# Step 1 of a batched FFT kernel: three fp16 products of a 98x98 matrix replaced by four 49x49 fp32 quarters of a folded input

## The chip, the cores and the metric

The kernel runs on one core of a Trainium2 chip. Its engines work side by side, each through its own fixed list of instructions: TensorE (PE in the profile) for matmuls, VectorE (DVE), ScalarE (ACT) and GpSimd (POOL) for elementwise work, and SyncE (SP), whose queue issues nearly all DMAs here. The metric is the device time of one execution in microseconds.

## What is computed

Eight batches of 3136 x 256 numbers go through a real FFT along the 3136 axis, a complex 256x256 mix with a bias, a soft threshold, the inverse FFT, and then a token-wise block with two matmuls (256 to 1024 and back):

```python
X = np.fft.rfft(x, axis=1)                      # x: (8, 3136, 256)
Yr = Xr @ w_r - Xi @ w_i + b_r
Yi = Xr @ w_i + Xi @ w_r + b_i
Y  = soft(Yr, 0.01) + 1j * soft(Yi, 0.01)       # sign(v) * max(|v| - 0.01, 0)
y  = np.fft.irfft(Y, n=3136, axis=1)
h  = y @ w_in;  sm = softmax(h);  solu = h * sm
out = (layernorm(solu) * g_ln) @ w_out
```

## The kernel before

3136 is 98 x 32, and the transform is done in two steps. **Step 1** multiplies x, seen as 98 rows (n1) of 32 x 256 columns, by a 98x98 matrix of cosines and sines. **Step 2** (`fwd2`) multiplies, for every pair of frequencies, by a 64-row matrix that holds the twiddle factors. The mix (`mix`), the threshold, step 3 (`inv1`, the inverse of step 2) and step 4 (`inv2`, the inverse of step 1) follow; between steps 1 and 2 and between 3 and 4 the numbers go through DRAM (`s1`, `s2`) to be turned. The token block is `moe_head` (first matmul, softmax), `moe_turn` (split into two fp16 parts, transposed by DMA) and `moe_tail` (second matmul, output).

Precision near fp32 is had from fp16 matmuls: a number is split into a high and a low half, and three products are added (high by high, low by high, high by low). A number must be scaled first so that fp16 holds it. So for batches three to eight (`b >= PLAIN`, which is 2) x is read twice: `load_peak` (L567) reads it in eight pieces of 128x784 to find its largest value, `x_scale` (L574) makes a power of two of it, and `fwd1` (L636) reads it again in eight chunks of 98x1024, splits each on ACT (`xh`) and DVE (`xl`), multiplies both halves of 512 columns three times by the matrix `fa16_s`, splits each product again on ACT and DVE into `av`, and stores it as fp16 pairs. `load_bin` (L702) then brings those pairs in ready for step 2. Batches one and two take `fwd1_plain` (L664): x is read once, multiplied in fp32 by `fa_s` with no scale, and the split is made after step 1, in `load_bin`.

Engines' lists are not in the order of the code. The kernel records every operation with a key (`nc.key`) and its needs; a planner (`Plan.order`, L365) walks through modelled time, and at each moment an engine takes, of the operations that could start within 50 ns of the first, the one with the lowest key. `weigh` (L319) sets an operation's modelled length: for TensorE it is divided by the number of array pieces that work at once (`op.half`: 2 for step 2, 8 for step 3). `banks` (L492) shares PSUM's eight banks out: `front_psum` and `inv2` use the name `pf` with at most five, `moe_head` `ph` with five, `moe_tail` `po` with two. All operations are issued by one helper line, so the profile's rows have L363 throughout, and groups are told apart by their tiles. Keys of step 1 come from `front_a` (L1282), those of steps 2 and 3 from `front_b` (L1292), from numbers at the end of the kernel.

In the rows `xt` is x as loaded, `bin` the input of step 2, `fb` and `gb` the matrices of steps 2 and 3, `w_hi`, `Xh` and `Xl` the mix, `th` and `tl` the two halves of the token block's transposed activations, `pf`, `ph` and `po` PSUM.

## Time and profile before

| | us |
|---|---|
| median of 3 runs | 1533.49 (1532.99 to 1537.09) |
| span of the profiled execution, first to last instruction | 1529.5 |
| PE busy | 1500.7 (98%) |
| DVE busy | 1285.7 (84%) |
| ACT busy | 1240.2 (81%) |
| POOL busy | 1143.4 (75%) |

The profile gives no time for its execution beyond the span, so the span stands for it: it is 4.0 us below the median of the runs, which is what lies around it there (start and end of the execution). A busy share is an average over the span; the same engine can be idle in one stretch and full in another, which the views by stretch show. Matmuls overlap, and their ends are modelled: how long one takes in a stream is read from the distance between starts, not from its duration.

### The profile page before, as it was taken

The numbers are of one execution on the slowest core, as the hardware profiler recorded it, in microseconds if no ns is written. First come the engines' busy times: TensorE is split into PE (matmuls) and PEld (weight loads), VectorE is DVE, ScalarE is ACT, GpSimd is POOL, SyncE is SP. The second block draws the span as 40 slices with busy tenths as digits, with TensorE's granted clock in tenths as the row PEclk, the third lists the DMA queues.
The fourth block names the chain that finished last, engine by engine and source line by source line (L and its number), as shares of the span: only waits on it lengthen the run. The fifth ranks groups of instructions, "written<-read, shape, count | busy, mean of one in ns | idle before, by whom it ended". The sixth has DMA issues, their size and how long they took to land.

```text
span 1529.5 us, 42136 instructions
## 1 busy us (share of the span) xinstructions
PE 1500.7 (98%) x15375; PEld 1061.3 (69%) x15375; DVE 1285.7 (84%) x3076; ACT 1240.2 (81%) x2532; POOL 1143.4 (75%) x1848
## 2 busy tenths in 40 slices
PE   6979999999999999999999999999999999999998
PEld 3436777677766777677766777667776677766766
DVE  5898898989898998989889898898979888776764
ACT  6778887987898778987888877897879788788886
POOL 0558987778966887678876788668986699867776
PEclk8989999999999999999999999999999999999999
DMA  8789866998699976999869996799969976687766
GB/s 267 219 265 211 166 129 128 254 222 222 131 216 233 224 165 127 235 230 227 155 140 238 232 202 143 160 236 230 199 135 201 208 161 121 138 173 141 149 124 115
DMA packets 531588, 285.69 MB, mean 187 GB/s; under 512 B 426500, under 2 KB 504688, under 8 KB 531380
## 3 DMA queue, kind: packets, MB, share of 16 engines
q1 hardware_dynamic: 530932, 281.39, 83.6%
q8 instruction: 120, 1.97, 0.5%
q10 hardware_dynamic: 448, 1.61, 0.4%
q14 instruction: 88, 0.72, 0.1%
HBM read 103.07 MB, written 77.07 MB: 118 GB/s over the span
## 4 chain that ended last, share of the span: by engine, by line
PE 86%; DVE 5%; ACT 3%; DMA 2%; POOL 2%; issue 1%; SPq 0%; DVEq 0%; ACTq 0%; POOLq 0%
PE ph L363 30%; PE po L363 30%; PE pf L363 24%; PE pb L363 2%; DMA tl<-ll 1%; DVE u L363 1%; DMA u<-in_x_dram 1%; DVE xl L363 1%; DVE nm L363 1%; ACT u L363 1%; DMA s<-av 0%; POOL ll L363 0%; DVE peaks L363 0%; SPq L363 0%; ACT lh L363 0%
## 5 line engine op out<-in xcount | busy, mean ns | idle before, releaser
L363 POOL TENSOR_TENSOR ll<-u,lh 128x1024 f16<-128x1024 f32 x196 | 421.4, 2150 | 103.7 <-ACT lh L363 96.0
L363 PE MATMUL po<-wout,th 128*128 128x256 f16 x3136 | 374.5, 273 | 0.0
L363 ACT ACTIVATE u<-ph,m,hsb 128x512 f32<-128x512 f32 x384 | 297.1, 780 | 80.6 <-DVE m L363 79.7
L363 PEld LDWEIGHTS <-th 128*128 128x128 f16 x3136 | 303.9, 98 | 58.7 <-issue 1.8
L363 DVE TENSOR_REDUCE nm<-ph 128x1 f32<-128x512 f32 x392 | 266.0, 688 | 89.2 <-PE ph L363 87.0
L363 DVE SCALAR_TENSOR_TENSOR u<-ph,ch,u 128x512 f32<-128x512 f32 x392 | 285.5, 748 | 46.9 <-ACT u L363 36.9
L363 PE MATMUL ph<-win_hi,ring_hi 128*128 128x512 f16 x768 | 291.3, 379 | 0.4 <-DVE u L363 0.3
L363 PE MATMUL ph<-win_low,ring_lo 128*128 128x512 f16 x768 | 291.0, 379 | 0.0
L363 PE MATMUL ph<-win_lo,ring_hi 128*128 128x512 f16 x768 | 291.0, 379 | 0.0
L363 ACT CAST lh<-u 128x1024 f16<-128x1024 f32 x196 | 206.5, 1054 | 67.1 <-DVE u L363 63.9
L363 PEld LDWEIGHTS <-ring_hi 128*128 128x128 f16 x1536 | 148.6, 98 | 138.1 <-issue 2.2
L363 ACT ACTIVATE junk<-u,total 128x1024 bf16<-128x1024 f32 x196 | 227.4, 1160 | 9.5 <-POOL total L363 8.4
L363 PE MATMUL po<-wout,tl 128*128 128x256 f16 x1568 | 203.4, 273 | 1.3 <-DMA tl<-ll 1.3
L363 PEld LDWEIGHTS <-tl 128*128 128x128 f16 x1568 | 151.7, 98 | 27.6 <-DMA tl<-ll 2.8
L363 POOL TENSOR_TENSOR y<-yt,yc 128x512 f32<-128x512 f32 (+1 forms) x104 | 132.0, 1274 | 26.1 <-DVE yc L363 20.7
L363 PE MATMUL pf<-w_hi,Xh 128*128 128x256 f16 x532 | 145.0, 273 | 0.1
L363 PE MATMUL pf<-w_hi,Xl 128*128 128x256 f16 x532 | 145.0, 273 | 0.0
L363 PE MATMUL pf<-w_lo,Xh 128*128 128x256 f16 x532 | 145.0, 273 | 0.0
L363 PEld LDWEIGHTS <-ring_lo 128*128 128x128 f16 x768 | 75.1, 98 | 90.7 <-DVE ring_lo L363 0.2
L363 PEld LDWEIGHTS <-Xh 128*128 128x128 f16 x1168 | 113.2, 98 | 35.5 <-issue 5.7
L363 POOL TENSOR_TENSOR yl<-y,yh 128x512 f16<-128x512 f32 x96 | 112.7, 1178 | 17.7 <-ACT yh L363 17.4
L363 POOL TENSOR_TENSOR r<-r,mhalf 128x1 f32<-128x1 f32 x196 | 113.2, 578 | 12.6
(204 smaller groups left out, 2699.0 us busy)
## 6 DMA issues: line engine op xcount, KB each, us to landing
xt<-in_x_dram SPq DMA_DIRECT2D x104, 392.0 KB
zt<-s SPq DMA_DIRECT2D x56, 392.0 KB
s<-zout SPq DMA_DIRECT2D x42, 512.0 KB
s<-av SPq DMA_DIRECT2D x48, 392.0 KB
bin<-s SPq DMA_DIRECT2D x36, 512.0 KB
out_dram<-o SPq DMA_DIRECT2D x128, 96.0 KB
out_dram<-o SPq DMA_DIRECT2D x136, 64.0 KB
out_dram<-o SPq DMA_DIRECT2D x128, 32.0 KB
```

What stands on the lines that cost most here:

```text
L363: getattr(engine, name)(*args, **kw)
```

## The change

From batch three on step 1 becomes `fwd1_fold`. A cosine row of the 98x98 matrix has the same value at n and n + 49 for an even frequency and the opposite one for an odd frequency; so has a sine row. The rows n and n + 49 of x are therefore added (`both`) and subtracted (written over the second half of `xf`), and each result is multiplied by a 49x49 matrix of its own (`fq_s`), in fp32 and without a scale. Two chunks of 1024 columns are taken together: four half chunks of 512 columns, each with a sum and a difference, make eight matmuls, and these are placed in four 64x64 pieces of the array by `tile_position`. The products leave PSUM by one ACT copy for each bank of 512 columns and are stored in fp32 (128 rows, of which 98 are used). `load_bin` and `fwd2_last` take the form that batches one and two have: they load fp32 and split it on ACT and DVE, now from two DMAs (four for `bin_s`) for one. `load_peak` is gone: the largest value is found in `xf`, and `x_scale` comes after step 1. x is loaded in 48 + 1 rows for each of two half chunks, four DMAs a chunk, into four buffers `xf` that stay in place; `clear_pads` fills the unused rows 49 to 63 and 113 to 127 of them once. `bin` has four buffers, where it had three.

The keys are new throughout: one table by kind of work, shifts by batch and kind (`SHIFT`) and by tile (`ROLE`), and modelled matmul lengths 0.6% longer.

```diff
+    FQ = np.zeros((4 * N2, 2, 2 * N2))
+    for odd in range(2):
+        for c in range(H):
+            k1, im = (2 * (c // 2) + 2 - odd, c % 2) if c < 2 * Q else (H * odd, 0)
+            t = 2 * np.pi * ((np.arange(H) * k1) % N1) / N1
+            for r in range(2):
+                FQ[r * 2 * N2 : r * 2 * N2 + H, odd, c] = -np.sin(t) if im else np.cos(t)
...
+KEYS = {
+    "fa": -300, "bias": -162.48, "start": 0, "warm": -200, "plain": -200, "weights": -161.13, "consts": -100,
...
+SHIFT = {
+    "inv24": 0.3, "inv21": 0.73, "a3": 0.8, "inv25": -0.83, "inv22": -2.27, "a5": 2.48, "a2": -3.15,
...
-            op.half = 8 if "gb" in ins[0].tile.kw["name"] else 2 if moving.tile.kw["name"][:2] == "fb" else 0
-            op.length += n / max(op.half, 1)
+            op.half = 8 if "gb" in lhs else 4 if lhs == "fq_s" else 2 if moving.tile.kw["name"][:2] == "fb" else 0
+            op.length += self.PACE * n / max(op.half, 1)
...
-    def fwd1(b, c):
...
+    def fwd1_fold(b, c0):
+        if c0 == 0:
+            s1[b] = dram.tile([P, N2, D], F32, name="s1")
+        half, rows = 2 * N2, 2 * N2 + H
+        v = x[b].rearrange("(h p n) d -> p h (n d)", h=2, n=N2)
...
+        for c in (c0, c0 + 1):
+            xt = xf[c % 4].rearrange("p (h m) -> p h m", h=2)
+            for r in range(2):
+                ms = slice(c * C1 + r * HF, c * C1 + (r + 1) * HF)
+                for p, n in ((0, H - 1), (H - 1, 1)):
+                    nc.sync.dma_start(xt[r * half + p : r * half + p + n], v[p : p + n, :, ms])
+            note_peak(b, c, NCH, xf[c % 4][:rows])
+            both = xp.tile([P, HF], F32, name="both")[:rows]
+            nc.vector.tensor_add(both, xt[:rows, 0], xt[:rows, 1])
+            nc.vector.tensor_sub(xt[:rows, 1], xt[:rows, 0], xt[:rows, 1])
+            folds.append((both, xt[:rows, 1]))
+        avs = [xp.tile([P, C1], F32, name="av", bufs=2) for _ in folds]
+        pas = [[front_psum(b) for _ in range(2)] for _ in folds]
+        nc.reserve(*avs)
+        with nc.together():
+            for fold, pa in zip(folds, pas):
+                for r in range(2):
+                    for odd in range(2):
+                        nc.tensor.matmul(
+                            pa[r][odd * half : (odd + 1) * half],
+                            fq_s[r * half : r * half + H, odd],
+                            fold[odd][r * half : r * half + H],
+                            start=True,
+                            stop=True,
+                            tile_position=(r * half, odd * half),
+                        )
+        for c, av, pa in zip((c0, c0 + 1), avs, pas):
+            for r in range(2):
+                nc.scalar.copy(av[:, r * HF : (r + 1) * HF], pa[r])
+            nc.sync.dma_start(s1[b][:, c * n2 : (c + 1) * n2], av.rearrange("p (n d) -> p n d", d=D))
...
-            t = fp.tile([P, QG, 2, D], F16, name="bin", bufs=3)
-            nc.sync.dma_start(t.rearrange("p q t d -> p q (t d)"), v[:, g * QG : (g + 1) * QG])
-            return t
...
+            t = fp.tile([P, QG, D], F32, name="bin", bufs=4)
+            half = 2 * N2
+            for odd in range(2):
...
+                nc.sync.dma_start(t[(1 - odd) * half : (2 - odd) * half], v[:, g * QG : (g + 1) * QG])
...
-        steps = [(load_peak, (b, c)) for c in range(NPK)] + [(x_scale, (b,))] + [(fwd1, (b, c)) for c in range(NCH)]
+        steps = [(fwd1_fold, (b, c)) for c in range(0, NCH, 2)] + [(x_scale, (b,))]
```

How the lists move is shown at one place of three engines, before and then after; an "x2" stands for that many equal rows. On PE, the first chunk of step 1 of batch three before, as it stands between a first token matmul (`ph`) and the mix: six products with `fa_s` (the fp16 matrix `fa16_s`), each with its weight load.

```order
L363 MATMUL pf<-xh,fa_s 98x512
L363 LDWEIGHTS fa_s
L363 MATMUL pf<-xh,fa_s 98x512
L363 LDWEIGHTS fa_s
L363 MATMUL pf<-xl,fa_s 98x512
L363 LDWEIGHTS fa_s
L363 MATMUL pf<-xh,fa_s 98x512
L363 LDWEIGHTS fa_s
L363 MATMUL pf<-xh,fa_s 98x512
L363 LDWEIGHTS fa_s
L363 MATMUL pf<-xl,fa_s 98x512
L363 LDWEIGHTS Xh_4384
```

Now, at the second group of step 1 by the new list, behind the second matmul of a token tile (`po`); a fp32 matmul is one row here that brings its own weights.

```order
L422 LDWEIGHTS tl
L422 MATMUL po<-wout,tl 128x256
L422 MATMUL pf<-both,fq_s 64x512
L422 MATMUL pf<-xf_101,fq_s 64x512
L422 MATMUL pf<-both,fq_s 64x512
L422 MATMUL pf<-xf_101,fq_s 64x512
L422 MATMUL pf<-both,fq_s 64x512
L422 MATMUL pf<-xf_118,fq_s 64x512
L422 MATMUL pf<-both,fq_s 64x512
L422 MATMUL pf<-xf_118,fq_s 64x512
L422 LDWEIGHTS Xh_3827
L422 MATMUL pf<-w_hi,Xh_3827 128x256
```

Two chunks are one group of eight rows where one chunk was six rows and as many weight loads; `both` and the difference (`xf`) alternate, first rows 0 to 48 of the array and then 64 to 112, and the same four pieces once more for the second chunk.

On DVE, in the middle of step 1 of batch three before, with rows of the token block (`u`, `nm`, `m`, `ch`) between them.

```order
L363 SCALAR_TENSOR_TENSOR xl<-xt,sc,xh 98x1024
L363 TENSOR_SCALAR ch<-m 128x1
L363 TENSOR_SCALAR ch<-ch,hsb 128x1
L363 SCALAR_TENSOR_TENSOR u,su_7861<-ph,ch,u 128x512
L363 SCALAR_TENSOR_TENSOR u,su_7870<-ph,ch,u 128x512
L363 SCALAR_TENSOR_TENSOR av<-pf,av 98x2x256 x2
L363 SCALAR_TENSOR_TENSOR xl<-xt,sc,xh 98x1024
L363 TENSOR_REDUCE nm<-ph 128x1 x2
```

And now at the last pair of chunks of step 1 of a batch.

```order
L422 TENSOR_REDUCE peaks<-xf_118 113x1
L422 SCALAR_TENSOR_TENSOR u,su_8351<-ph,ch,u 128x512
L422 TENSOR_TENSOR both<-xf_101 113x512
L422 TENSOR_REDUCE top<-peaks 113x1
L422 TENSOR_TENSOR xf_101<-xf_101 113x512
L422 TENSOR_TENSOR both<-xf_118 113x512
L422 TENSOR_REDUCE nm<-ph 128x1
L422 TENSOR_TENSOR xf_118<-xf_118 113x512
```

The splits of x (`xl`) and of the product (`av`) have left; the reduction for the largest value (`peaks`), the sum and the difference stand there, and `x_scale` (`top`) behind the last reduction.

On SP's queue before, where x of the next batch is read for its largest value and for step 1 and `bin` is loaded between them.

```order
L363 DMA xt<-in_x_dram 128x784 x3
L363 DMA_TRANSPOSE tl<-ll 128x8x128
L363 DMA bin<-s_7995 128x4x512
L363 DMA_TRANSPOSE th<-lh 128x8x128
L363 DMA bin_s<-s_7995 64x256 x2
L363 DMA xt<-in_x_dram 128x784
L363 DMA out_dram<-o 64x256 x2
L363 DMA xt<-in_x_dram 98x1024
```

And now, at the end of the loads of one batch and the start of its `bin`.

```order
L422 DMA xf_86<-in_x_dram 48x2x512
L422 DMA xf_86<-in_x_dram 1x2x512
L422 DMA s_6129<-av 128x1024
L422 DMA xf_86<-in_x_dram 48x2x512
L422 DMA s_6129<-av 128x1024
L422 DMA xf_86<-in_x_dram 1x2x512
L422 DMA_TRANSPOSE th<-lh 128x8x128
L422 DMA out_dram<-o 64x256 x2
L422 DMA_TRANSPOSE tl<-ll 128x8x128
L422 DMA zt<-s_6847 98x2048 x2
L422 DMA_TRANSPOSE th<-lh 128x8x128
L422 DMA bin<-s_6129 64x4x256 x2
```

A chunk of x is two rows of 48 and two of 1 partition where it was one row and one for the peak, and a `bin` is two rows of 64 partitions where it was one of 128.

## Rows read from the trace of the kernel before

**Rows 1.** The page of the kernel before: busy time of each engine with its share of the span, and two rows of the forty slices (PE's busy tenths, and the granted TensorE clock in tenths of full speed).
```profile
PE 1500.7 (98%) x15375; PEld 1061.3 (69%) x15375; DVE 1285.7 (84%) x3076; ACT 1240.2 (81%) x2532; POOL 1143.4 (75%) x1848
...
PE   6979999999999999999999999999999999999998
...
PEclk8989999999999999999999999999999999999999
```

**Rows 2.** The page's chain of work that ended last: shares of the span by engine.
```profile
PE 86%; DVE 5%; ACT 3%; DMA 2%; POOL 2%; issue 1%; SPq 0%; DVEq 0%; ACTq 0%; POOLq 0%
```

**Rows 3.** Stretches of the span, all engines: start:end and length in us, then busy us of PE, PEld (weight loads), DVE, ACT and POOL with their numbers of instructions, the granted clock, the mean busy share of the 16 DMA engines and GB/s.
```profile
0.00:100.00 100.00, 84.31 (x843) 41.42 (x844) 75.89 (x146) 71.68 (x136) 42.34 (x41) 0.91 0.78 240
100.00:200.00 100.00, 93.18 (x804) 67.08 (x803) 87.03 (x223) 80.02 (x171) 79.36 (x122) 0.97 0.92 203
...
800.00:900.00 100.00, 99.81 (x1030) 71.57 (x1029) 93.67 (x206) 81.92 (x169) 74.18 (x118) 1.00 1.07 242
...
1400.00:1529.00 129.00, 124.54 (x964) 87.50 (x961) 80.43 (x216) 98.96 (x200) 90.04 (x178) 0.99 0.71 131
```

**Rows 4.** PE's instructions in order of time around the first chunk of step 1 of batch three, and the two that follow it (start us, us until the modelled end of the last, operation, shapes, number of instructions).
```profile
256.52 0.60 PE L363 MATMUL pf<-xh,fa_s 98*98 98x512 f16 x2
256.96 0.38 PE L363 MATMUL pf<-xl,fa_s 98*98 98x512 f16 x1
257.17 0.59 PE L363 MATMUL pf<-xh,fa_s 98*98 98x512 f16 x2
...
257.82 0.27 PE L363 MATMUL pf<-w_hi,Xh 128*128 128x256 f16 x1
...
259.13 1.91 PE L363 MATMUL po<-wout,th 128*128 128x256 f16 x16
```

**Rows 5.** The same view of PE at one chunk of step 1 of batch two, which is already multiplied in fp32 (two matmuls of 512 columns, which the trace records as four), and the next instruction.
```profile
57.14 1.88 PE L363 MATMUL pf<-xt,fa_s 98*98 98x512 f32 x4
58.86 0.38 PE L363 MATMUL pb<-w_hi,Xh 128*128 128x512 f16 x1
```

**Rows 6.** The same view of PE at a group of step 3 (tile `gb`, 96 matmuls on eight 32x64 pieces of the array; its first 16 and last 16) and what follows it, then at a group of step 2 (tile `fb`, 96 matmuls of 64 columns on two 64-row pieces) with the rows on both sides.
```profile
260.97 0.42 PE L363 MATMUL pf<-yh,gb 32*64 32x256 f16 x16
...
262.08 0.40 PE L363 MATMUL pf<-yh,gb 32*64 32x256 f16 x16
262.42 1.05 PE L363 MATMUL po<-wout,tl 128*128 128x256 f16 x8
...
514.83 1.91 PE L363 MATMUL po<-wout,th 128*128 128x256 f16 x16
516.67 1.57 PE L363 MATMUL pf<-fb,bin 64*128 64x64 f16 x96
518.17 1.05 PE L363 MATMUL po<-wout,tl 128*128 128x256 f16 x8
```

**Rows 7.** DVE's instructions grouped by operation and shape: out<-in, out shape<-in shape, number, busy us in all and mean ns of one, idle time before them.
```profile
L363 DVE SCALAR_TENSOR_TENSOR xl<-xt,sc,xh 98x1024 f16<-98x1024 f32 x48 | 64.9, 1351 | 0.1
L363 DVE SCALAR_TENSOR_TENSOR av<-pf,av 98x512 f16<-98x512 f32 x96 | 63.0, 686 | 7.1 <-ACT av L363 7.1
L363 DVE TENSOR_REDUCE peaks<-xt 128x1 f32<-128x784 f32 x48 | 46.0, 962 | 0.1
L363 DVE TENSOR_REDUCE peaks<-xt 98x1 f32<-98x1024 f32 x12 | 14.5, 1210 | 9.3 <-DMA xt<-in_x_dram 9.3
L363 DVE SCALAR_TENSOR_TENSOR bin<-bin,sc 128x1024 f16<-128x1024 f32 x6 | 8.1, 1356 | 0.4 <-ACT bin L363 0.4
L363 DVE SCALAR_TENSOR_TENSOR u<-u,junk 128x512 f32<-128x512 uint32 x4 | 2.7, 683 | 0.0
L363 DVE SCALAR_TENSOR_TENSOR bin_s<-bin_s,sc,bin_s 64x256 f16<-64x256 f32 x2 | 1.0, 484 | 0.1
L363 DVE TENSOR_SCALAR un<-pf 128x2 f32<-128x2 f32 x7 | 1.1, 159 | 4.8 <-PE pf L363 4.7
```

**Rows 8.** The same view of ACT.
```profile
L363 ACT ACTIVATE xh<-xt,sc 98x1024 f16<-98x1024 f32 x48 | 54.9, 1162 | 1.2 <-DVE sc L363 1.1
L363 ACT ACTIVATE av<-pf 98x512 f16<-98x512 f32 x96 | 54.6, 603 | 4.7 <-PE pf L363 3.1 <-DMA s<-av 0.9
L363 ACT COPY av<-pf 98x512 f32<-98x512 f32 x16 | 9.0, 586 | 1.9 <-PE pf L363 1.1 <-DMA s1f<-av 0.8
L363 ACT ACTIVATE bin<-bin,sc 128x1024 f16<-128x1024 f32 x6 | 7.2, 1197 | 0.0
L363 ACT ACTIVATE bin_s<-bin_s,sc 128x256 f16<-128x256 f32 x2 | 1.2, 598 | 0.0
```

**Rows 9.** The same view of PE: the matmuls of step 1 on the second half of x, and the last column tells what PE waited for before them in the whole run.
```profile
L363 PE MATMUL pf<-xl,fa_s 98*98 98x512 f16 x96 | 36.3, 378 | 0.6 <-DVE xl L363 0.6
```

**Rows 10.** DMA: the page's count of packets; issues by tile with their number and size; and, from the views of the tiles `xt` and `tl`, the time that one issue takes on SP's queue (ns min/median/max).
```profile
DMA packets 531588, 285.69 MB, mean 187 GB/s; under 512 B 426500, under 2 KB 504688, under 8 KB 531380
...
xt<-in_x_dram SPq DMA_DIRECT2D x104, 392.0 KB
s<-av SPq DMA_DIRECT2D x48, 392.0 KB
...
L363 SPq DMA_DIRECT2D xt<-in_x_dram x104: 316/500/1904, 46.5 to 1172.8; - x104
...
L363 SPq DMA_TRANSPOSE tl<-ll x196: 1231/1248/3634, 134.7 to 1521.2; - x196
```

More of the change, by code (lines that the diff above doesn't have):

```diff
@@ L241, in tile @@
         return View(t, (0, 128), np.arange(512), F32)
+KEYS = {
+    "fa": -300, "bias": -162.48, "start": 0, "warm": -200, "plain": -200, "weights": -161.13, "consts": -100,
+    "groups": 0, "x0": -197.18, "y0": -78.59, "b0": -110.81, "b0s": 7.792, "w_in0": -138.86, "w_in1": -62.72,
+    "w_in": -46.29, "w_out0": -26.19, "w_out": -16.44, "mix": 13.09, "pads": -16.1, "a1": -43.04, "a1s": 5.385,
+    "a2": 4.85, "a2s": 4.919, "a": 4.52, "b1": 3.41, "b1s": 0.904, "b": -21.55, "bs": 1.176, "inv2": -2.03,
+    "turn": 12.26, "tail": 4.37, "as": 3.466,
+}
@@ L244, with first_tile, key_of, __init__ @@
+def first_tile(b):
+    return 24 * b + b // 2
+def key_of(stage, b=0, n=0, keys=KEYS):
+    if stage in ("a", "b"):
+        name = f"{stage}{b}" if f"{stage}{b}" in keys else stage
+        step = keys[f"{name}s"]
+        at = first_tile(b - 1 if stage == "b" else b - 2) if b > (stage == "a") else 0
+        return at + keys[name] + n * step
+    if stage in ("inv2", "head", "turn", "tail"):
+        return first_tile(b) + n + keys.get(stage, 0)
+    return keys[stage]
 class Op:
-    def __init__(self, engine, key, seq):
-        self.engine, self.key, self.seq = engine, key, seq
+    def __init__(self, engine, stage, role, seq):
+        self.engine, self.stage, self.seq = engine, stage, seq
+        self.key = key_of(*stage) + SHIFT.get("".join(map(str, stage[:2])), 0) + ROLE.get(f"{stage[0]}/{role}", 0)
@@ L271, in __init__, with at @@
     def __init__(self, nc):
-        self.nc, self.ops, self.key, self.group, self.held, self.reserved = nc, [], 0.0, None, (), ()
+        self.nc, self.ops, self.stage, self.group, self.held, self.reserved = nc, [], ("start",), None, (), ()
         for e in self.ENGINES:
             setattr(self, e, _Engine(self, e))
+    def at(self, *stage):
+        self.stage = stage
     def together(self):
@@ L290, in take @@
         if op is None or op is True:
-            op = Op(engine, self.key, len(self.ops))
+            role = args[0].tile.kw["name"] if isinstance(args[0], View) else "out"
+            op = Op(engine, self.stage, "D" * (name == "dma_start") + role, len(self.ops))
             self.ops.append(op)
@@ L472, in fft_mix_solu_kernel @@
 @with_exitstack
-def fft_mix_solu_kernel(ctx: ExitStack, tc, x, w_r, w_i, b_r, b_i, w_in, w_out, g_ln, fa, iaf, fa16, fb, fs, gb, gs, ia, out):
+def fft_mix_solu_kernel(ctx: ExitStack, tc, x, w_r, w_i, b_r, b_i, w_in, w_out, g_ln, fa, fq, none, iaf, fb, fs, gb, gs, ia, out):
     nc = Plan(tc.nc)
@@ L510, in fft_mix_solu_kernel @@
         nc.sync.dma_start(bias_row[:, r], v.unsqueeze(0))
-    nc.key = 0
+    nc.at("start")
     ident = const.tile([P, P], F32, name="ident")
@@ L558, in load_after @@
         nc.sync.dma_start(t, src)
+    xf = [const.tile([P, C1], F32, name=f"xf{i}") for i in range(4)]
     peaks, scales = {}, {}
@@ new lines, in clear_pads @@
+    def clear_pads():
+        for t in xf:
+            for r in (0, 2 * N2):
+                nc.sync.dma_start(t[r + H : r + 2 * N2], none)
+    def fwd1_fold(b, c0):
[3 more added lines that the diff above has]
+        v = x[b].rearrange("(h p n) d -> p h (n d)", h=2, n=N2)
+        n2 = C1 // D
+        folds = []
+        for c in (c0, c0 + 1):
[28 more added lines that the diff above has]
+            nc.sync.dma_start(s1[b][:, c * n2 : (c + 1) * n2], av.rearrange("p (n d) -> p n d", d=D))
@@ L669, in fwd1_plain @@
         n2 = C1 // D
-        pool, name, bufs = (mp, "u", 4) if b == 0 and c % 2 == 0 else (xp, "xt", 4)
-        xt = pool.tile([P, C1], F32, name=name, bufs=bufs)[:N1]
-        if b and c < 4:
-            nc.hold(raw[0, 4])
+        if b:
+            xt = xf[c % 4][:N1]
+            if c < 4:
+                nc.hold(raw[0, 4])
+        else:
+            xt = xf[c // 2][:N1] if c % 2 else mp.tile([P, C1], F32, name="u", bufs=4)[:N1]
         queue = nc.scalar if b == 0 and c % 2 else nc.sync
@@ L1192, in fft_mix_solu_kernel @@
     iaf_s = const.tile([N1, N1], F32, name="iaf_s")
-    fa16_s = const.tile([N1, 2, N1], F16, name="fa16_s")
+    fq_s = const.tile([P, 2, 2 * N2], F32, name="fq_s")
     ia_s = const.tile([N1, 3, N1], F16, name="ia_s")
-    nc.key = 0
+    nc.at("groups")
     fb_s, gb_s = {}, {}
@@ L1297, in front_b @@
         for n in range(NU + lag):
-            nc.key = key + n * step
+            nc.at("b", b, n)
             for fn, m in ((fwd2, n), (mix, n - 1)):
```

147 lines of the change are left out of this document (66 added, 81 removed).

## The prediction

> **What bounds the kernel now.** I read the busy times first: PE is busy 1500.7 of 1529.5 us, no other engine over 84% [rows 1]. Then the chain of work that ended last: 86% of it is PE [rows 2]. Then the stretches: PE misses 15.7 us of the first 100 us and 6.8 of the second, from there at most a few tenths in 100 us, at the full granted clock, and 4.5 us at the end; that makes 22.5 of its 28.8 idle us in the first 200 [rows 1, 3]. So behind 200 us a microsecond of PE's work that goes, or comes, moves the end by a microsecond, unless another engine fills the place; the fullest, DVE, reaches 93.7 in the stretch from 800 to 900 us [rows 3]. PE does not wait on step 1's inputs either: before the matmuls of `xl` it lost 0.6 us in the whole run [rows 9]. The question is thus what step 1 costs PE before and after.
>
> A single profiled execution gives these rows: span 1529.5 us. The median of the runs is 1533.49, so I add each sum to 1533.5 and take the 4.0 us around the span as unchanged.
>
> **PE, removed.** One chunk of step 1 (six fp16 matmuls of 512 columns) goes from 256.52 to 257.82 us, where the mix begins: 1.30 us [rows 4]. Two chunks, which the change takes together, are 2.60 us; six batches of four pairs make 24 pairs: 62.4 us.
>
> **PE, added.** fp32 stands in the trace on the whole array: two matmuls of 98x98 by 512 columns from 57.14 to 58.86 us, 1.72 us, recorded as four passes of 0.43 us, so 0.86 us for one matmul [rows 5]. A pair now has eight matmuls of 512 columns on four pieces of the array. If the four pieces stream side by side, each has two: 2 x 0.86 = 1.72 us.
>
> No row shows fp32 in pieces, but two show fp16 in them. Twelve matmuls of 256 columns go from 257.82 to 259.13 us, 0.109 us each [rows 4]. The 96 of a step 3 group would take 10.5 us in single file; they take 1.45 us, 260.97 to 262.42 [rows 6]. Eight abreast they are twelve deep, 1.31 us, and 0.14 us is left over at the way out; 16 matmuls from 259.13 end at 260.87, so another 0.10 us is lost at the way in [rows 4, 6]. Step 2, two abreast: 96 of 64 columns are 48 deep at a quarter of 0.109, 1.31 us, and take 1.50 (516.67 to 518.17); the way in is 0.10 again (16 from 514.83 end at 516.57), so 0.29 us in all against 0.24 [rows 6]. Between the two I take 0.26 us for a group on four pieces.
>
> New group: 1.72 + 0.26 = 1.98 us. Saved: 2.60 - 1.98 = 0.62 us, 24 times: 14.9 us.
>
> Both ends of the unknown: perfect overlap with no switching cost is 1.72 us a pair, a gain of 21.1 us; eight matmuls in single file are 6.88 + 0.26 = 7.14 us, a loss of 109 us. I take four abreast, because the nearest rows (pieces of the same array, of 32 and of 64 rows) run at their full number abreast. One thing differs, and it decides the first rival below: in steps 2 and 3 neighbouring matmuls go to different pieces, while a fp32 matmul is two passes [rows 5], and both must go to the same piece.
>
> **DVE.** Removed: 46.0 (peaks of 784 columns) + 64.9 (`xl`) + 63.0 (`av`) = 173.9 us [rows 7]. Added: 48 reductions of 1024 columns at 1.21 = 58.1; 96 sums and differences of 512 columns, which no row shows, at 0.68 by the nearest, a two-input fp32 instruction of 512 columns, = 65.6; 36 splits of `bin` at 1.356 = 48.8; 6 of `bin_s` at 0.484 = 2.9 [rows 7]. Together 175.4 us: 1.5 more, beside PE. For the sums and differences the ends are 0.48 us (half of a 784-column reduction) and 0.69 (`av`, which reads PSUM), so DVE's total changes by -18 to +2 us over six batches, none of it on the path while DVE has 6 us in 100 free in its fullest stretch [rows 3, 7].
>
> **ACT.** Removed 54.9 + 54.6 = 109.5 us; added 96 copies at 0.586 (56.3), 36 `bin` at 1.197 (43.1), 6 `bin_s` at 0.598 (3.6): 103.0 us, 6.5 less [rows 8]. POOL gets no instruction and loses none.
>
> **DMA and SP's queue.** x is read once: 48 loads of 392 KB go, 19.3 MB; the fp32 store has 128 rows where 98 stood, 120 KB more in each of 48, 5.9 MB. Net -13.4 of 285.7 MB [rows 10]. Issues: per batch 32 loads of x for 16, 12 of `bin` for 6, 4 of `bin_s` for 2, so 24 more, 144 for six batches, and 8 for the pads: 152 at 0.50 us = 76 us more on SP, whose transposes take 392 x 1.25 = 490 us of the 1529 [rows 10]. What is queued behind a late issue there is a transpose, and behind that the second token matmul on PE. A thousand other issues at 0.50 us would still leave SP over 500 us of the span, so I price it at nothing; without that cover a transpose is late by the four issues of a chunk, 2 us. Whether loads in 2 KB runs take longer to land than in 4 KB runs no row shows; between a gain of a few us (the stretch from 800 to 900 us has its DMA engines full, 1.07 [rows 3]) and a loss of as many I take nothing.
>
> **What moves.** Step 1 no longer waits for the scale, and `x_scale` comes behind it. Its small DVE-PE-DVE steps (`un` waited 4.8 us for PE in seven batches [rows 7]) now stand ahead of the first `bin` split. The lists put a stretch of token work there, which hides them; bare, they would cost about 1 us a batch, 6 us. The first group of step 1 of batch three stands much earlier on PE, in the stretch where PE has holes. With new keys those 22.5 idle us can shrink or grow; the rows give no direction, so nothing in the sum, and up to half of them, 11 us, either way in the range. No stall is removed after 200 us; what would be late next is DVE, whose share rises by the 1% that the span shrinks.
>
> **Sum.** 1533.5 - 14.9 = 1518.6 us.
>
> **Rival 1, the two passes hold the line (slower).** If PE starts matmuls strictly in their order, the second pass of a matmul waits for the first on its piece, and the next matmul, though its piece is free, waits behind. Then each matmul sets the line back by one pass: 8 x 0.43 + 0.43 = 3.87, with the switch 4.13 us a pair, 1.53 more than before, 24 times 36.7 us: 1570.2 us. It decides as soon as a pair takes over 2.60 us, which is fewer than three pieces abreast. For it: the order `both`, difference, `both`, difference gives no two passes of different pieces as neighbours but at the seams. Against it: pieces 32 and 64 rows high run at their full number here [rows 6].
>
> The Trainium skill speaks on both sides. "TensorE: Matmul & The Clock Gate" (Part 3, The mechanism) says that matmuls start and end in program order, with no reordering, and that only weight loads are pulled ahead; taken literally, that is this rival and 1570 us. "TensorEngine Tiling (Array Packing)" (Key Properties) says that tiles run independently and load and multiply in parallel; that is the forecast. The rows of steps 2 and 3 agree with both, since no piece is used twice in a row there.
>
> **Rival 2, the gain is given back in waits (about the same).** A group now takes four of the five `pf` banks at once and holds them through four ACT copies of 0.59 us, where a half chunk took one [rows 8]; its eight matmuls start only when two chunks are summed and differenced. If the mix or step 4 behind it waits 0.62 us for each group, the gain is gone: 1533.5; at 0.9 us it is 1540. For it: DVE and ACT are over 80% full, and ACT's `av` waited for PE only 3.1 us, so the banks are turned over tightly [rows 1, 8]. Against it: step 3 takes four banks already, and PE shows no idle time around its group [rows 6].
>
> **Rival 3, no pieces at all.** fp32 in single file: 1533.5 + 109 = 1642 us. Only a rule against fp32 in pieces would do it; no row speaks for it.
>
> **Chances.** A change of 0.3% (4.6 us) is about what a measurement of this kernel can tell from none. Forecast 0.66, with its own range 1505 to 1528: the low end is the sum less half of the early idle time and some of the switching cost, the high end a few tenths of wait a group. Rival 1 0.16, rival 2 0.14 (1527 to 1540), rival 3 0.01, and 0.03 for an early stretch that loses more than all the rest gains. The range 1505 to 1540 holds the forecast and rival 2, some 0.80; rival 1 lies outside. Faster (under 1528.9): the forecast and a little of rival 2, 0.69. Within 0.3%: most of rival 2, 0.11. Slower: rivals 1 and 3 and the rest, 0.20.
>
> **What the profile after will show.** Right: a group of 16 passes on `fq_s` (eight matmuls) between its first start and the next instruction's in 1.9 to 2.1 us; PE busy near 1486 us and its idle time still under 30 us; DVE within 5 us of 1286, ACT some 6 under 1240; 272 MB moved. Wrong by rival 1: 4.1 us a group with starts 0.43 us apart. Wrong by rival 2: groups of 2.0 us, with idle time of PE in front of them or behind them, put down to ACT `av` or DVE `xf`. Most directly, the forecast falls if a group takes over 2.6 us.

## The result, and the profile after

The changed kernel takes 1544.3 us (median of 4 runs, 1542.6 to 1544.5) where the kernel before takes 1533.4 beside it: ratio 1.0069, 95% interval 1.0054 to 1.0084. It is 0.7% slower. The forecast was 1518.6 us, 1% faster, and the range ended at 1540. All ratios below are to runs of the kernel before on the same chip, 1532.0 to 1533.0 us each time, with their 95% interval behind them; two ratios whose intervals overlap are not told apart. One execution of `e11_x64_bin1` (1724.4 us) and one of `e18_single3` (3130.2 us) took far longer than the others of the same kernel and are left out of what is given for these two.

The page of the kernel after, busy time and DMA packets; its span is 1542.3 us.
```profile
PE 1495.1 (97%) x15471; PEld 1036.9 (67%) x15471; DVE 1299.9 (84%) x3070; ACT 1228.4 (80%) x2526; POOL 1164.0 (75%) x1848
...
DMA packets 533014, 273.26 MB, mean 177 GB/s; under 512 B 427676, under 2 KB 505992, under 8 KB 532804
```
PE is busy 5.6 us less than in [rows 1] and idle 47.2 us instead of 28.8. The bytes fell by 12.4 MB [rows 10]. So the kernel moves less, multiplies less and takes longer: the loss is waiting.

PE after, in order of time, at one group of step 1 (two chunks, eight matmuls, recorded as 16 passes; this answers to [rows 4, 5]), and the token matmul that follows.
```profile
442.45 0.64 PE L422 MATMUL pf<-both,fq_s 49*64 49x512 f32 x1
442.45 0.64 PE L422 MATMUL pf<-xf,fq_s 49*64 49x512 f32 x1
442.46 0.64 PE L422 MATMUL pf<-both,fq_s 49*64 49x512 f32 x1
442.47 0.64 PE L422 MATMUL pf<-xf,fq_s 49*64 49x512 f32 x1
442.93 0.59 PE L422 MATMUL pf<-both,fq_s 49*64 49x512 f32 x1
...
443.36 0.59 PE L422 MATMUL pf<-both,fq_s 49*64 49x512 f32 x1
...
443.79 0.59 PE L422 MATMUL pf<-both,fq_s 49*64 49x512 f32 x1
...
444.33 0.39 PE L422 MATMUL ph<-win_hi,ring_hi 128*128 128x512 f16 x1
```
Four passes start within 20 ns, then four more, four times over; the next instruction starts 1.88 us after the first. So it is in 23 of the 24 groups; one takes 1.94 us.

The stretches after, columns as in [rows 3]: then the same two stretches before, and of the run without the added DMAs (`e17_noone_bin1`, below).
```profile
150.00:400.00 250.00, 245.98 (x2680) 177.75 (x2679) 219.63 (x508) 205.17 (x418) 205.47 (x313) 1.00 0.82 178
400.00:1250.00 850.00, 835.45 (x8937) 583.47 (x8936) 744.27 (x1763) 686.30 (x1423) 660.23 (x1055) 1.00 0.85 181
```
```profile
150.00:400.00 250.00, 249.44 (x2862) 184.73 (x2860) 223.31 (x519) 207.32 (x429) 206.71 (x313) 1.00 0.84 183
400.00:1250.00 850.00, 849.02 (x8917) 610.67 (x8916) 747.79 (x1785) 705.56 (x1444) 651.68 (x1060) 1.00 0.89 194
```
```profile
150.00:400.00 250.00, 246.35 (x2687) 178.33 (x2686) 221.78 (x512) 206.15 (x422) 206.52 (x312) 1.00 0.85 180
400.00:1250.00 850.00, 846.34 (x9138) 594.80 (x9137) 752.81 (x1792) 700.12 (x1451) 674.81 (x1076) 1.00 0.85 184
```
From 400 to 1250 us, where 19 of the 24 groups stand, PE now misses 14.6 us where it missed 1.0; from 150 to 400 it is 4.0 for 0.6. A matmul's end is modelled, so some lost time counts as busy. From start to start (each gap less the shortest usual gap between two such matmuls) PE's work fell by 13 to 16 us, and the time lost beside it rose by 26 to 29 us, depending on what is taken for usual.

What the engines wait for, after (us in all, times, longest), the rows that end in a DMA:
```profile
DVE peaks L422 <- DMA xf<-in_x_dram: 27.0, 16, 4.8
...
ACT bin L422 <- DMA bin<-s: 12.4, 11, 1.9
POOL ll L422 <- DMA tl<-ll: 11.4, 8, 3.5
PEld L422 <- DMA tl<-ll: 6.1, 8, 1.1
```
and the same view before, where `bin` is not among them:
```profile
DVE peaks L363 <- DMA xt<-in_x_dram: 9.3, 4, 4.1
POOL ll L363 <- DMA tl<-ll: 6.3, 8, 1.8
PEld L363 <- DMA tl<-ll: 3.2, 5, 1.1
```
All rows of that view that end in a DMA, without the `zt` loads, sum to 25.5 us before and 72.3 after. (Of the 27.0 us for x, 12.2 lie in the first 150 us.) One such place, SP's issues and then DVE's instructions with their wait:
```profile
353.55 2.36 SPq L422 DMA_DIRECT2D xf<-in_x_dram  x4
356.01 0.87 SPq L422 DMA_DIRECT2D s<-av  x2
356.93 2.82 SPq L422 DMA_DIRECT2D xf<-in_x_dram  x4
```
```profile
359.72 1.22 DVE L422 TENSOR_REDUCE peaks<-xf 113x1 f32<-113x1024 f32 x1 [2.64 <-DMA xf<-in_x_dram]
...
364.61 1.22 DVE L422 TENSOR_REDUCE peaks<-xf 113x1 f32<-113x1024 f32 x1 [1.40 <-DMA xf<-in_x_dram]
```
A chunk of x is now four issues, over 2 us of SP, and DVE, which stands still until the last of them has landed, goes on 3.8 and 4.9 us after their end.

The trace records each arrival of a DMA, so landing can be read. Median us from the end of the issue to the last arrival, with the arrivals that one DMA makes:
```
x, 48 rows of a quarter (after)    3.6   16 arrivals
x, the single row (after)          3.0    3
x, 49 rows in one (e5_x49)         5.3    8
x, 64 rows in one (e10_x64)        4.4   16
bin, half of 64 rows (after)       3.5   16
bin, 128 rows in one (e9_bin1)     3.9   16
```
The trace also has how far ahead of its first use a load is issued (medians, least in brackets). Before, a piece of the extra reading of x was issued 9.5 us (4.7) ahead of its peak reduction, and needed 4.6 us from issue to last arrival. x for step 1 was issued 41.8 us (11.1) ahead of its split, since that waited for the scale. After, one reading serves both: the peak reduction comes 7.8 us (4.4) after the first issue of a chunk, which needs 6.7 us to its last arrival, and the sum 49.6 us (10.0) after it. The first user of `bin` was PE, 18.9 us (6.8) after the issue; now it is ACT's split, 6.5 us (4.8) after it, and in 17 of 36 places ACT begins less than 0.2 us after the last arrival.

DVE's times did not move the end (`e3_nopeak`, below): these are its groups after that answer to [rows 7].
```profile
L422 DVE SCALAR_TENSOR_TENSOR bin<-bin,sc 128x1024 f16<-128x1024 f32 x42 | 58.4, 1390 | 2.1 <-ACT bin L422 2.0
L422 DVE TENSOR_REDUCE peaks<-xf 113x1 f32<-113x1024 f32 x48 | 58.1, 1211 | 15.7 <-DMA xf<-in_x_dram 15.6
...
L422 DVE TENSOR_TENSOR xf<-xf 113x512 f32<-113x512 f32 x48 | 39.9, 834 | 0.0
L422 DVE TENSOR_TENSOR both<-xf 113x512 f32<-113x512 f32 x48 | 34.3, 730 | 0.0
```

### The profile page after: what moved, and what is told of

The parts are those of the page before. It is cut to its first block, busy times and chain, and to the rows that moved or that the text cites. A ratio compares the mean times of both kernels' runs of the same rounds, so it can differ in the third digit from the quotient of the medians.

```text
span 1542.3 us, 42453 instructions
## 1 busy us (share of the span) xinstructions
PE 1495.1 (97%) x15471; PEld 1036.9 (67%) x15471; DVE 1299.9 (84%) x3070; ACT 1228.4 (80%) x2526; POOL 1164.0 (75%) x1848
## 3 DMA queue, kind: packets, MB, share of 16 engines
q8 instruction: 121, 1.98, 0.5%
## 5 line engine op out<-in xcount | busy, mean ns | idle before, releaser
L422 POOL TENSOR_TENSOR y<-yt,yc 128x512 f32<-128x512 f32 (+1 forms) x104 | 135.1, 1303 | 40.6 <-ACT yt L422 25.0
L422 POOL TENSOR_SCALAR se<-se,se 128x1 f32<-128x1 f32 x196 | 67.0, 342 | 96.2 <-ACT u L422 67.5
```

The source lines that it names most:

```text
L422: getattr(engine, name)(*args, **kw)
```

## The experiments

Except where it says otherwise an edit keeps the changed kernel's order: the planner works as it did, and instructions are exchanged or left out afterwards. The edits are shown shortened, with the run's name as a comment where a cut holds several.

### Is it the new order, DVE's amount, or the planner's price of a DMA?

`e1_oldkeys` folds, with the keys of before and no shifts; `e3_nopeak` leaves out 42 of the 48 peak reductions of the folded batches (their scale comes from the first chunk alone); `e4_dma600` lets the planner count 600 ns for an issue.
```diff
-        self.key = key_of(*stage) + SHIFT.get(...) + ROLE.get(...)
+        self.key = key_of(*stage)                 # e1, key_of with the numbers of before
+        op.skip = b >= PLAIN and c > 0            # e3, in note_peak
-            op.length += 1600.0 if cross else 430.0
+            op.length += 1600.0 if cross else 600.0   # e4
```


> The folded step 1 as it is, but every key is that of the kernel before (a pair of chunks stands where its chunks stood on average, the scale at the end of the batch's step 1; no shifts by batch, kind or tile). Theory K (the new keys put step 2 of a batch close behind its step 1, so that its splits and waits lie bare on PE): the 0.63 us a group comes through, 1519 to 1526 us, PE's lost time behind 200 us back from about 24 to under 8 us. Theory S (SP's queue, with 152 more issues, brings x late) and theory D (DVE has too much to do beside steps 1 and 2): both are in this kernel too, so 1540 us or more.

> The changed kernel with the same order on every engine, but 42 of 48 reductions for the largest value of x are left out of DVE's list (the scale comes from the first chunk alone): 51 us less on DVE, 8.5 a batch, all in the stretch of step 1. Theory D: PE's lost time falls by 10 us or more, 1534 or less. Theory S: the wait for x only passes to the sum that follows, 1541 or more. Theory K: 1538 to 1544.

> The changed kernel, with the planner's modelled issue of a DMA raised from 430 to 600 ns (the trace shows 585 for x), so that it orders with SP's time as it is. Theory S: the loads are placed earlier or their users later, 1538 or less. Theories K and D: within 4 us of 1544, either way.

Measured: 1557.6 us (1.0157, 1.0140 to 1.0175), 1547.3 (1.0098, 1.0081 to 1.0115) and 1555.4 (1.0149, 1.0124 to 1.0174). The new keys are not the loss: the fold without them is 13 us worse. DVE was 42 us less busy (1257.9) in the second and nothing was won, so its amount is not the bound. The third made another order and a worse one, which no theory of its expectation had.

### Fewer DMAs for x

`e2_noone` leaves out 88 of the 96 single-row loads (row 49 of each quarter then holds old data); `e5_x49` loads the 49 rows by one DMA; `e6_act1` issues the single rows on ACT's queue; `e10_x64` loads 64 rows by one DMA, in batches three to seven.
```diff
                 for p, n in ((0, H - 1), (H - 1, 1)):
+                    op.skip = n == 1 and (b > PLAIN or c > 3)                                      # e2
+                    n > 1: op.calls[0] = "dma_start", (xt[r * half : r * half + H], v[0:H, :, ms]), {}   # e5; n == 1: op.skip = True
+                    if n == 1: op.queue = "scalar"                                                 # e6
+                    more = bass.AP(x.tensor, at, [[N2 * D, half], [H * N2 * D, 2], [1, HF]])       # e10
```


> The changed kernel with the same order on every engine, but the loads of single rows of x (88 of 200 issues of x on SP) are left out after the first four chunks, so rows 48 and 97 of x are stale: part of the computation is left out. SP loses about 51 us of issues. Theory S: DVE's wait for x falls from 15.6 us behind 200 us to under 5, and the time by 8 us or more, to 1536 or less. Theories K and D: within 3 us of 1544.

> The changed kernel with the same order on PE, DVE, ACT and POOL, but 49 rows of x go by one DMA where there were one of 48 and one of 1: 96 issues less on SP, about 56 us, every byte still loaded. Theory S (SP's issues): 1533 to 1538 us, as in the run without the single rows. Theory B (what that run won was the bytes or packets left out, which are all here again): 1541 or more.

> The changed kernel, in which the 96 loads of single rows are issued by ACT's queue instead of SP's, at their old place in the plan: the same DMAs, 56 us less on SP and as much more on ACT, which is 80% busy. Theory S (SP's issues): 1533 to 1541 us, the gain of the run without single rows less what ACT loses. Theory R (single-row DMAs, or the packets that they put before others, are themselves late): 1543 or more.

> The changed kernel in the same order, but for batches two to six each quarter of x is loaded by one DMA of 64 rows (15 rows more than are used, 30% more bytes) in place of one of 48 rows and one of a single row: 80 issues fewer. Theory S (issues): -7.5 us, 1535 to 1539 us. Theory L (what made one DMA of 49 rows 18 us slower is the number of rows: 49 rows come over fewer DMA rings than 48, and 64 rows do not): the same 1535 to 1539 and the wait of VectorE for x at or below the 14.8 us of the changed kernel; if one DMA for a whole quarter is slow whatever its rows: 1555 or more.

Measured: 1536.1 us (1.0023, 1.0013 to 1.0033), 1562.0 (1.0191, 1.0173 to 1.0209), 1547.7 (1.0099, 1.0078 to 1.0121) and 1549.3 (1.0108, 1.0092 to 1.0124). Leaving 88 DMAs out wins 7 us, but 96 and 80 fewer issues lose 19 and 6 where the load that is left lands later after its issue (5.3 and 4.4 us, table above), and issues moved from SP to ACT win nothing. So fewer issues on SP do not win by themselves. What one issue costs `e6_act1` does not tell, since SP there waited for DMAs itself, 60 us in 65 places where it was 33 us in 31. The fourth run came as none of its theories had it. From the first issue of a chunk to its last arrival it is 6.7 us (median) in the changed kernel, 7.4 in `e5_x49`, and 6.5 in `e10_x64` and `e2_noone`: only with 49 rows is a chunk complete later, and what cost `e10_x64` 6 us is not shown.

The chain of waits shows where the late loads go, here from 330 to 640 us of `e5_x49`, with three of its pieces (start us, us):
```profile
by line: PE pf L422 20.2%; PE po L422 16.5%; PE ph L422 16.1%; DMA bin<-s 10.3%; DMA xf<-in_x_dram 6.3%; issue 4.6%; DMA th<-lh 2.3%; POOL ll L422 2.3%; SPq L422 2.2%; ACT u L422 2.0%; ACT lh L422 1.7%; DVE bin L422 1.3%; ACT bin L422 1.2%;
...
356.57 10.55 DMA xf<-in_x_dram
...
494.12 6.99 DMA bin<-s
...
511.58 7.72 DMA bin<-s
```
The loads of x and of `bin` are links of the chain that sets the end. In [rows 2] all DMA together were 2%. In the changed kernel itself the chain from the end breaks off at 1097 us. Followed back by the same rule from PE's last matmul that begins before 1080 us, it has 67 us of DMA between 330 and 1080 us (x 20.8, `bin` 19.7, the transposes 16.3) and 26 us of SP's issues. The kernel before has 18 us of DMA there, none of it x or `bin`, and 5 of issues, `e17_noone_bin1` (below) 10 and 1.

A load of 49 rows makes 8 arrivals and the single row 3. "DMA: Bandwidth & Descriptors" of the Trainium skill (Why a DMA increments its semaphore by 16 and not by 1) says that a copy is spread over the largest number of engines up to 16 that divides the slowest dimension of both its sides, and that the issuing queue writes the rest of the 16 counts; by it 49 rows use seven engines and a single row of two halves two. The 8 and 3 arrivals agree, if what the queue writes is recorded as one.

### One load for step 2's input

`e7_x49_bin` is the 49-row kernel, `e9_bin1` the changed one, `e11_x64_bin1` the 64-row one, each with one DMA of 128 rows for `bin`; step 2 then reads its rows in another order, the same amount.
```diff
             for odd in range(2):
-                nc.sync.dma_start(t[(1 - odd) * half : (2 - odd) * half], v[:, g * QG : (g + 1) * QG])
+                odd == 0: op.calls[0] = "dma_start", (t, whole[:, g * QG : (g + 1) * QG]), {}      # odd == 1: op.skip = True
```


> As the run with 49 rows, and bin of batches three to eight also comes by one DMA of 128 rows where there were two of 64; the rows that it brings are not the right ones (part of the computation is changed), bytes and order are the same. 36 more issues less on SP, about 24 us. Theory S: another 2 to 5 us less than with 49 rows alone, 1529 to 1534. If SP was relieved enough already: within 1.5 us of it.

> The changed kernel with every other order as it is, but step 2's input of batches two and up (`bin`) loaded by one DMA of 128 rows instead of two of 64, 36 issues fewer; the rows it reads are in another order, so the values are wrong, and the amount of data is the same. Theory S (the issues on SP are the price, whichever they are): leaving 88 issues out gave 8.2 us, 0.093 us each, so 36 give about 3.4: 1539 to 1542 us. Theory B (each `bin` half is late by itself, since two DMAs must both land; with the 49-row loads the one DMA gave back 16.3 us): 1525 to 1533. If neither: 1543 to 1546.

> Both together, 116 issues fewer, rows of step 2 in another order as in the run with `bin` alone. Theory S: -10.8 us, 1531 to 1535 us. If the two prices add up as one and the same queue: the sum of what the two runs gave, within 2 us. If VectorE's amount or the order is what holds it: not under 1538.

Measured: 1545.7 us (1.0086, 1.0058 to 1.0114), 1534.4 (1.0014, 1.0005 to 1.0023) and 1541.9 (1.0058, 1.0038 to 1.0078). The 36 DMAs are worth 8 us on the changed kernel, three times as much apiece as the single rows, 16 on the 49-row one and 8 on the 64-row one; whether the other order of the rows has a share in it is not tried. The first gained over three times what its theory had, the second came just above the range of its better theory, and for the third the two effects add up (1.0053 by the other ratios). In the stretch shown above the chain of `e9_bin1` has no DMA in it:
```profile
by line: PE pf L422 22.4%; PE po L422 20.5%; PE ph L422 20.4%; issue 5.9%; POOL ll L422 3.5%; ACT u L422 2.9%; POOL r L422 2.2%; DVE xf L422 2.1%; ACT lh L422 1.8%; DVE nm L422 1.6%; DVE u L422 1.6%; POOL y L422 1.2%; DVE Xl L422 1.2%; POOL
```
One whole load lands no sooner after its issue (3.9 us) than a half does (3.5), but from the first issue to the last arrival two halves take 5.3 us and the whole 4.5: what is saved is the second. "DMA: Bandwidth & Descriptors" of the Trainium skill (Rules for kernel authors) advises one 128-partition transfer over two halves, since both halves run on the same engines. The 8 us agree.

### Is SP off the path?

`e8_dup1` issues each of the 88 single-row loads twice.
```diff
+                    if n == 1 and (b > PLAIN or c > 3): op.calls.append(op.calls[0])
```


> The changed kernel with 88 of its single-row loads issued twice on SP (the same rows to the same place): 51 us more issues on SP, 0.36 MB more. Theory S: the loss grows by about what leaving them out won, 1549 to 1556. If SP were not on the path: within 2 us of 1544.

Measured: 1768.6 us, ratio 1.154, far over both theories. SP waits for the first load of a row before it issues the second:
```profile
SPq L422 <- DMA xf<-in_x_dram: 210.9, 91, 5.1
```
This is not the price of an issue that was meant, but it tells more: SP stood still for 211 us in 91 places, about 2.3 us each, and the end moved by some 224.
```profile
PE 1563.2 (88%) x15471; PEld 1064.3 (60%) x15471; DVE 1298.9 (74%) x3070; ACT 1231.7 (70%) x2526; POOL 1159.4 (66%) x1848
```
Of the 224 us PE was idle for 157 more and busy for 68 more with the same matmuls: with its longer waits the granted clock was 0.95 from 150 to 400 us, 0.94 to 900 and 0.93 to 1450, where it was 1.00 in the changed kernel. So most of SP's standing still came through to PE, in stalls of 2.3 us: behind a waiting issue stand the next transpose and the next load. Whether a shorter stall would be hidden this run does not tell.

### Would a later first use help?

`e13_late6` and `e14_late12` put DVE's peak reduction of a chunk up to six or twelve DVE instructions later, `e15_late6_bin2` also ACT's first use of `bin` two later, `e16_late6_bin1` is the first with one DMA for `bin` (rows in another order). No load moves.
```diff
+        op.later = 6 * (b >= PLAIN)      # note_peak; e14: 12; e15: also 2 on ACT's bin
+            while to < len(order) and left and order[to] not in op.next and not set(op.tiles) & set(order[to].tiles):
```


> The changed kernel with one edit to its order: the peak reduction of each folded chunk, VectorE's first use of x, stands up to six VectorE instructions later (not past its own chunk's sum); every load, every other instruction and all other engines' orders stay. Theory L (x's four loads land after VectorE's order has come to them, and the engine stands still until they do): the wait of VectorE for x falls from 27.0 us to about 12 to 15, of which 11 belong to batch two, and the time by 6 to 10 us: 1534 to 1538. Theory P (the engine would wait for something else next, the PE's lateness is set by the transposes alone): within 2 us of the changed kernel, 1542 to 1547.

> The same with up to twelve instructions. Theory L: the wait for x falls a little further, the time is within 2 us of the run with six. Theory P: 1542 to 1547.

> The run with six, and the first use of step 2's input on ScalarE (`bin` to fp16) up to two instructions later too. Theory L, if it holds for `bin` as for x: ScalarE's wait for `bin` falls from 12.4 us to under 6 and the time by 2 to 5 us more, 1530 to 1535. If step 2 is needed at once by PE: no better than the run with six, or up to 3 us worse.

> The run with six, and `bin` by one DMA of 128 rows (the rows in another order, so the values are wrong). Theory L: both gains together, 1526 to 1531 us, below the kernel before. If both gains were one and the same wait: 1533 to 1536.

Measured: 1550.3 us (1.0110, 1.0088 to 1.0132), 1553.1 (1.0130, 1.0115 to 1.0145), 1556.5 (1.0151, 1.0134 to 1.0168) and 1541.8 (1.0055, 1.0036 to 1.0074). The waits went as foreseen, in `e13_late6` and `e15_late6_bin2`:
```profile
DVE peaks L431 <- DMA xf<-in_x_dram: 10.9, 5, 3.8
```
```profile
ACT bin L431 <- DMA bin<-s: 1.9, 2, 1.1
```
and yet both are slower than the changed kernel, `e15_late6_bin2` by most. None of the four came as expected, under either theory, in size. So taking the standing still of DVE and ACT away does not win its time. Why the shifted runs are slower is not shown. Step 1 itself does not wait for x: in the changed kernel the sum of a chunk starts 42 us (median) after the chunk has landed and 33 us after its peak reduction. Other waits grew in place of those that went, ACT's for `bin` to 16.0 us in `e13_late6`. That a wait is only a sign of when the data lands, and that this costs, is argued.

### Nearly all added DMAs out, 48 of them out, and another order

`e17_noone_bin1` joins `e2_noone` and `e9_bin1`, 124 DMAs fewer (old data in row 49, `bin`'s rows in another order). `e18_single3` loads the two single rows of a chunk by one DMA, 48 fewer. `e12_x64_plan` writes the 64-row loads into the program, so that the planner makes a new order.
```diff
+                        two = bass.AP(x.tensor, at, [[HF, 2], [H * N2 * D, 2], [1, HF]])           # e18
+                        op.calls[0] = "dma_start", (Raw(xt, "__getitem__", slice(H - 1, half + H, half)), two), {}
```


> The changed kernel in its own order, without the 88 single-row loads of x and with step 2's input by one DMA instead of two halves (48 rows of 49 are fresh and step 2 reads its rows in another order, so the values are wrong): 124 DMAs fewer of 1337. Theory C (the load of x, step 1, the store, the load of `bin` and step 2 are one chain beside TensorE that has no slack, and each DMA left out of it lets its data land sooner): both gains add up, 8.2 + 9.9 us below 1544.3, 1524 to 1529 us, under the kernel before. If both removed the same wait: 1532 to 1536.

> The changed kernel in its own order, with the two single rows of a chunk (row 49 of each quarter, 64 partitions apart) loaded by one DMA: three DMAs a chunk in place of four, 48 fewer, and all of x loaded. Theory C: about half of what leaving 88 out gave, 1538 to 1541 us. If the data must have left, not the DMA, to win time: 1543 to 1546.

> The 64-row loads again, but written so in the program, so that the planner sees 80 DMAs fewer and makes its own order from them. If the order of the changed kernel has no part in it: within 3 us of the run with the same loads in the old order. If each order is a draw of its own around the issue price (the planner with another price for a DMA was 11 us slower): off by over 3 us to either side.

Measured: 1530.8 us (0.9989, 0.9981 to 0.9998), 1538.4 (1.0040, 1.0027 to 1.0053) and 1573.4 (1.0254, 1.0227 to 1.0282). In the second the data was not all right, for a cause that was not found, so it counts for the number of its DMAs and is no version to use. The first is 12 us under the changed kernel by ratio, where the two parts alone give 7 and 8: two waits for the most part, not one. Its waits for x and the transposes:
```profile
DVE peaks L422 <- DMA xf<-in_x_dram: 13.3, 9, 3.6
...
POOL ll L422 <- DMA tl<-ll: 3.7, 3, 1.7
```
ACT's wait for `bin` is down to 0.7 us, and the sum over all rows that end in a DMA is 26.2 us, as before the change (25.5). The third is 22 us slower than the same loads in the old order: an order is a draw of its own here, larger than the whole change. Four orders of the folded step 1 were run (the changed kernel, `e1_oldkeys`, `e4_dma600`, `e12_x64_plan`), all slower than the kernel before; whether another one would bring the gain is not tried.

Over the runs that keep the order and the first uses, the sum of DMA waits goes with the time, `e6_act1` apart, and the number of DMAs that SP and ACT issue does not:
```
run              DMAs   waits ended by a DMA, us   ratio to before
e17_noone_bin1   1213    26.2                      0.9989
e9_bin1          1301    41.7                      1.0014
e2_noone         1249    42.1                      1.0023
e18_single3      1289    47.0                      1.0040
e11_x64_bin1     1221    58.0                      1.0058
changed kernel   1337    72.3                      1.0069
e7_x49_bin       1205    69.9                      1.0086
e3_nopeak        1337    77.8                      1.0098
e6_act1          1337    64.7                      1.0099
e10_x64          1257    79.1                      1.0108
e5_x49           1241   100.5                      1.0191
```

This goes together, but it does not prove that the waits are the price: the four runs with a later first use have 39 to 66 us of them at 1.0055 to 1.0151.

No run came 0.3% under the kernel before; the one just below it leaves rows of x out.

## Why the prediction was wrong, step by step

**PE, removed and added: right.** The 1.98 us counted the way in, which the 1.88 from start to start leave out: the matmul ahead of a group takes 0.09 us longer than usual to the next start (0.203 us for 0.109 at 256 columns, 0.309 for 0.216 at 512). Together that is 1.97, and 15 us are saved. PE's busy time, whose ends are modelled, fell by 5.6 us and not by these 15, so it was no sign to go by.

**Rivals 1 and 3: false.** Two passes of one matmul do not hold the line: passes of four pieces start together. Read literally, the rule on program order in "TensorE: Matmul & The Clock Gate" of the Trainium skill (Part 3, The mechanism) gave 4.13 us a group. The rows with 20 ns between four starts contradict that reading, at least for the passes. They agree with "TensorEngine Tiling (Array Packing)" of the Trainium skill (Key Properties), by which tiles work in parallel.

**DVE and ACT: off, and without effect as far as tried.** DVE's total rose by 14.2 us, outside the -18 to +2 that was given. The usual sum and difference took 0.68 us as taken (medians 682 and 681 ns), but seven of the 96 took 1.1 to 2.6 us, which makes the means 730 and 834; why is not shown. ACT fell by 11.8, not 6.5. DVE's amount does not decide (`e3_nopeak`).

**DMA and SP's queue: the step that failed.** It put the bytes right (-12.4 MB for -13.4) and priced 152 issues at nothing because SP had 500 us free over the span, and the landing of shorter runs at nothing for want of a row. An average hid the stretch: from 353.6 to 359.8 us, above, SP issues without a gap, and in `e8_dup1` its stalls of 2.3 us come through for the most part. With the cover gone the step allowed "late by the four issues of a chunk, 2 us"; it did not count that this comes 48 times, and that `bin` in two halves comes on top. What the runs show in place of nothing: taking 124 of the added DMAs out (`e17_noone_bin1`) gives 0.8%, 12 us, back and brings the waits that end in a DMA from 72.3 us to 26.2. How the 12 us divide between SP's time, the landing and the limit of eight DMAs under way (last section) is open.

**What moves: the leads.** This step said nothing of how far ahead of its first use a load stands. For x itself the freedom was real: the sum comes 49.6 us after the first issue, where the split came 41.8 after it. But the peak reduction now waits for four issues, with 7.8 us of lead over 6.7 of landing where it had 9.5 over 4.6, and `bin` has 6.5 us to ACT's split where it had 18.9 to PE. The leads before can be read from the trace before and were not. No run changes a lead alone, so what each costs is not shown.

**Early part: the open rest.** From the forecast (0.9903 of before) to `e17_noone_bin1` (0.9989) 13 us are missing. By starts, PE had lost 10 us more there than before by the 33rd `po` group on `tl` (395 us), and some 5 more after that. Seven of the ten are lost by the first of these groups, at 150 us (139 before). At most 5 of them are the granted clock, an estimate: up to 121 us PE had the lower level (1.2 of 2.4 GHz) for 34 us in `e17_noone_bin1`, 31 in the changed kernel and 24 before, and half of the 10 us more is 5. Before the level fell at 96 us PE had been busy for about 9 of 11.5 us in all three. Nothing for it stood in the sum, up to 11 us either way in the range. That the rest lies in the order of the start (keys, x's buffers shared with batch two) is argued, not shown: no run isolates it.

**Rival 2: right in kind, wrong in place.** The gain was given back in waits, at a cost of 1.1 us a group instead of the 0.9 that it named as its end. It looked at PSUM banks; but PE's trace after has no idle time before the groups on `fq_s`. The waits are in front of the mix, the tokens and step 2, where these three groups had 0.1, 1.3 and 0.0 us before:
```profile
L422 PE MATMUL pf<-both,fq_s 49*64 49x512 f32 x192 | 46.6, 602 | 0.0
L422 PE MATMUL pf<-xf,fq_s 49*64 49x512 f32 x192 | 46.6, 602 | 0.0
...
L422 PE MATMUL pf<-w_hi,Xh 128*128 128x256 f16 x532 | 145.1, 273 | 4.5 <-DVE Xs L422 1.6 <-ACT Xh L422 0.7 <-DVE zout L422 0.7
L422 PE MATMUL po<-wout,tl 128*128 128x256 f16 x1568 | 203.4, 273 | 3.2 <-DMA tl<-ll 3.2
L422 PE MATMUL pf<-fb,bin 64*128 64x64 f16 x2016 | 34.2, 190 | 4.5 <-DVE ring_lo L422 1.6 <-DVE ch L422 1.5 <-DVE u L422 1.1
```
A chance of 0.14 for a give-back was far too low for a change that puts 152 more DMAs into a queue whose free time was known only on average.

## What to carry over

When a change takes work off the bounding engine, list for every load that it adds, splits or gives another first user how far ahead of that use it is issued, and compare this lead with issue plus landing; a queue with free time on average may have none where it counts. One load of `bin` beat two halves, but one load of 49 or 64 rows of x lost to 48 rows and one: measure when the last arrival comes, and do not only count issues. A wait seen on a helper engine need not be the price: shift its first use before you believe that it is.

## What was not expected of the hardware

- fp32 matmuls of 49x64 on four pieces run four abreast, pass by pass: 16 passes in four rounds, 0.43 to 0.48 us apart, 1.88 us in all, and 0.09 at the way in.
- A load of 49 rows lands 5.3 us after its issue, one of 48 rows 3.6, one of 64 rows 4.4 with 30% more bytes.
- From the start of an issue to its last arrival, never more than eight of the DMAs issued by SP and ACT were under way: 44 us with eight after, 18 before. An issue whose predecessor eight earlier was still out began within 0.1 us of that one's last arrival, 37 times after and 11 before. Whether this limit, which may be the program's own eight semaphores, costs part of the 12 us was not tried by itself.
- Leaving out issues does not free SP by their time: with 80 fewer (`e10_x64`) its issues took 1068 us in all, for 1062, as a transpose took 1.48 us to issue, in the mean, instead of 1.41.
